# A cached-attention and MLP decode kernel: a folded weight's two halves loaded at the very first on two queues, and one scalar put behind the last gelu

## The chip, the cores and the metric

The kernel runs on one core of a Trainium2 chip. Its engines are TensorE (PE, with its weight loads listed apart as PEld), VectorE (DVE), ScalarE (ACT), GpSimd (POOL) and SyncE (SP), and 16 DMA engines carry what the queues of SP and ACT issue. The metric is the device time of one execution in microseconds; lower is better. Before the change three runs took 1078.3, 1078.7 and 1079.33 us, median 1078.7 us.

## The reference, cut to what matters

Two layers are run, each an attention block A followed by an MLP block B, with the same weights in both layers. There are 8 rows (batch), one token each, width D = 448, 16 query heads over 8 key/value heads, 4096 cached positions of 256 elements, all bf16:

```python
x = A_x
x = x + _A_ref(_layernorm(x), A_k_cache, A_v_cache, A_wq, A_wo)
x = x + _B_ref(_layernorm(x), B_w1, B_w2, B_w3, B_w4)
x = x + _A_ref(_layernorm(x), A_k_cache, A_v_cache, A_wq, A_wo)
x = x + _B_ref(_layernorm(x), B_w1, B_w2, B_w3, B_w4)
```

`_A_ref` forms q = x @ wq, scores against the K cache, softmax over 4096 positions, the sum over the V cache, and `@ wo`. In `_B_ref` the token is one position long, so every shifted part of the first mixer is zero and `x1 = x`; what is left is `x + gelu(layernorm(x) @ w3) @ w4` with w3 of 448 x 1792 and w4 of 1792 x 448. The K and V caches together are 268 MB; each row's 33.5 MB are needed by both layers.

## The kernel before, in words

Each of the 64 (row, head) pairs has a K tile and a V tile of 2 MB, cut in four units of 512 KB ("u" 0 to 3, one SBUF slot each, 30 slots in all). A front (`front`) loads a K tile, transposes it on TensorE (L1509), copies it back (DVE L1440 or ACT L1441), takes the scores (L1148, L1405) and does the softmax; a back (`back`) loads the V tile, multiplies (L1275), sums the partial rows (L1311) and applies wo (L1339, L1086). Some units of heads 3 to 7 are kept in SBUF from layer 0 to layer 1; all others are read a second time. Row b+1's layer 0 is interleaved with row b's layer 1, and `mid` runs row b's layer-0 MLP in between. The first six rows share one MLP of the second layer; the last two rows have a last one at the very end (`mlp` with `dst is None`), whose output `last_rows` forms and stores.

The order of everything is worked out on the host by a planner, `Plan.schedule`. It is a list scheduler with a modelled duration for every operation: at each step the engine that can begin first takes its ready operation of the lowest `prio`. It gives slots to the K and V units and joins neighbouring units into one transfer of up to 2 MB; a transfer waits on its queue until the last reader of every slot that it overwrites is done. In gaps of TensorE's plan it puts filler matmuls (listed at L1716), so many that a modelled count of recent columns stays under a target. After it `synchronise` derives the semaphore waits. So a changed duration or dependency moves later decisions of the plan too.

Transfers on the SP queue go in order of `prio`. K and V units count 0, 1, 2, ... as they are called for; the constant weights stand between them by `at`:

```python
def dma_once(name, parts, keys, at, also=()):
    for i, (dst, src, nbytes, *row) in enumerate(parts):
        dma(name, dst, src, nbytes, nc.alloc_semaphore(f"s_{name}{i}"), 16,
            [keys[i], *(also if i == 0 else ())], 4 * at - 0.5, *row)
```

448 rows of a weight are three blocks of 128 and one of 64. The fourth block of wq and of w3 is folded: its left half of columns stands in partitions 0 to 63 of one tile and its right half in partitions 64 to 127 (`wqx_sb`, `w3x_sb`). Before the change the order on SP is: x, the left half of wqx, two K tiles, wq, more K and V, wo, K and V, and at `at` = 18 w3's three blocks and both halves of w3x (two transfers of 112 KB, L628), then V units and w4. The right half of wqx is the only load issued by ACT's queue, at the start (L1575). Who reads w3x: `column_sums_h` (L917, once, with the mask as the other operand) and the first product of every MLP (L917).

At the end of the last MLP (DVE): L1031 and L1033 form the argument of tanh, ACT does tanh (L1037), L1046 forms gelu times two (`hT`), which TensorE multiplies with w4 (L973). Beside it `last_scale(1)` works out two scalars of the last row's residual (L828; L830 and L836), with which L965 scales the residual `xs`; L979 adds the product and `xs`, and two transfers store the rows (L982).

Of the kernel before, what the change touches and what calls it, by code (L numbers as in the profile page):

```python
# [6 lines left out]
P = 128  # L7
B = 8
D = 448
# [466 lines left out]
def bass_interleave_layers__gqa_block_cached__mixer_s_mlp__decode_kernel(  # L476
# [20 lines left out]
    plan = Plan()  # L497
# [6 lines left out]
    def sb(name, shape, dt):  # L504
        n = 4 if dt in (f32, i32) else 2
        for s in shape[1:]:
            n *= s
        al = 32 if n >= 128 else 8
        cursor[0] = (cursor[0] + al - 1) // al * al
        t = nc.alloc_sbuf_tensor_at(name, shape, dt, offset=cursor[0], align_bytes=al)  # L510
        cursor[0] += (n + al - 1) // al * al
        assert cursor[0] <= high0, (name, cursor[0], high0)
        return t
# [5 lines left out]
    w3x_sb = sb("w3x_sb", [P, F // 2], bf)  # L519
# [31 lines left out]
    lin = sb("lin", [P, 2, 2], f32)  # L551
# [5 lines left out]
    hT = sb("hT", [P, NB], bf)  # L557
# [67 lines left out]
    def dma(name, dst, src, nbytes, sem, val, wr, at, row=8192):  # L625

        us = nbytes / 16 / 26.88e3 + nbytes / row / 16 * 0.008
        plan.op("sp", lambda eng: eng.dma_start(dst, src), us / FASTER, name, wr=wr, prio=at,  # L628
                dma=(sem, val))
# [6 lines that stand above are left out]
# [49 lines left out]
    def const_c(v):  # L685
# [7 lines left out]
            wr=["sel"])  # L693
# [7 lines left out]
    for bank, key in [(psR, "R"), (psM, M)]:  # L701
        plan.op("dve", lambda v, bank=bank: v.memset(bank[:, :], 0.0), 0.5, "const",
                wr=["psM", ("row", 0), ("row", 1)], banks=[key])
# [7 lines left out]
    def dv(fn, dur=0.13, rd=(), wr=(), banks=(), name="chain", prio=None):  # L711
        if prio is None:
            prio = urge[0] + len(plan.ops)
        return plan.op("dve", fn, dur, name, rd=rd, wr=wr, banks=banks, prio=prio)
# [71 lines left out]
    def factor(k, c, v, rd, dv=dv):  # L786


        x, t, y = (z[:, k, c:c + 1] for z in (var, rst, rsy))
        a, b = (KK * (1.0 + LN_EPS) / D, KK * LN_EPS * LN_EPS) if k else (KK / D, KK * LN_EPS)  # L790
        dv(lambda e: e.tensor_scalar(x, v, a, b, ALU.mult, ALU.add), rd=rd, wr=[("x", k, c)])
        newton(x, t, y, ("t", k, c), [("x", k, c)], ("y", k, c), dv)
# [26 lines left out]
    def last_scale(r):  # L819


        c = B - 2 + r
        y, sf = rsy[:, 0, c:c + 1], self_f[:, r:r + 1]
        mm = mom[:, 2, 4 * r + 1:4 * r + 2]
        if r == 0:
            factor(0, c, mom[:, 2, 4 * r:4 * r + 1], [("v", r)])
        add = self_f[:, 0:1] if r == 0 else lin[:, 0, 0:1]
        dv(lambda v: v.tensor_scalar(lin[:, r, 0:1], y, sf, add, ALU.mult, ALU.add),  # L828
           rd=[("y", 0, c), "sel_f"] + [("lin", 0, 0), "hT"] * r, wr=[("lin", r, 0)])
        dv(lambda v: v.tensor_scalar(lin[:, r, 1:2], y, sf, mm, ALU.mult, ALU.mult),  # L830
           rd=[("y", 0, c), ("mm", r), "sel_f"], wr=[("lin", r, 1)])
        if r == 0:
            dv(lambda v: v.tensor_tensor(lin[:, 0, 0:1], lin[:, 0, 0:1], self_f[:, 1:2], ALU.add),
               rd=[("lin", 0, 0), "sel_f"], wr=[("lin", 0, 0)])
        else:
            dv(lambda v: v.tensor_tensor(lin[:, 1, 1:2], lin[:, 1, 1:2], lin[:, 0, 1:2], ALU.add),  # L836
               rd=[("lin", 0, 1), ("lin", 1, 1)], wr=[("lin", 1, 1)])
# [148 lines left out]
    def mlp(src, skey, n, dst, dkeys, rows_open=False):  # L986
# [62 lines left out]
        if dst is None:  # L1049
            last_scale(1)  # L1050
            return last_rows(src, skey, n)
# [518 lines left out]
    def load_wq():  # L1570
        dma_once("wq", [(wq_sb[:, kc, :], A_wq[kc * P:(kc + 1) * P, :], 1 << 20)
                        for kc in range(3)], ["wq0", "wq1", "wq2"], 2)
        dma_once("wqx", [(wqx_sb[0:64, :], A_wq[384:D, 0:2048], 1 << 19)], ["wqx0"], 0.05)
        s_wqx = nc.alloc_semaphore("s_wqx1")
        plan.op("act", lambda a: a.dma_start(wqx_sb[64:P, :], A_wq[384:D, 2048:4096]), 0.1, "wqx1",  # L1575
                wr=["wqx1"], prio=0, dma=(s_wqx, 16))

    def load_rest():
        dma_once("wo", [(wo_sb[:, :].rearrange("p (t n) -> p t n", n=2 * D),
                         A_wo.rearrange("(t m c) n -> m t (c n)", m=P, c=2), 3670016, 1792)], ["wo0"], 6)  # L1580
        dma_once("w3", [(w3_sb[:, kc, :], B_w3[kc * P:(kc + 1) * P, :], 458752)
                        for kc in range(3)], ["w30", "w31", "w32"], 18)
        dma_once("w3x", [(w3x_sb[0:64, :], B_w3[384:D, 0:896], 114688 * 2),
                         (w3x_sb[64:P, :], B_w3[384:D, 896:1792], 114688 * 2)], ["w3x0", "w3x1"], 18)
    def load_w4():
        w4s = B_w4.rearrange("(s f) n -> s f n", s=2)
        dma_once("w4", [(w4_sb[:, 7 * i * D:(7 * i + 6) * D].rearrange("p (t n) -> p t n", n=2 * D),
                         w4s[i, 0:768].rearrange("(t m c) n -> m t (c n)", m=P, c=2), 688128, 1792)
                        for i in range(2)] +
                 [(w4_sb[:, (7 * i + 6) * D:(7 * i + 7) * D], w4s[i, 768:896], 114688, 896)  # L1590
                  for i in range(2)], ["w40", "w41", "w42", "w43"], 20, ["xr0", "xr1", "xr2"])
# [58 lines left out]
    def with_first_results(k, b):  # L1650
# [15 lines left out]
        run(k[MLP_TO:])  # L1666

    load_wq()
    load_rest()
    first_queries()  # L1670
    load_w4()
# [6 lines left out]
    for b in range(B):  # L1678
        kf = {"K": l2_heads[:], "F": free_heads[:]}
        order2 = [kf[c].pop(0) for c in MIX] if b < B - 2 else l2_heads + free_heads  # L1680
        first = QFIRST if b < B - 1 else QLAST
        mid(b, order2[:first])
        q_todo[b] = order2[first:]
        first2[b] = order2[0]
        if b < B - 1:
            run([("b", 0, b + 1, h) for h in free_heads])
        if b < B - 2:
            run(both(1, b, order2))
            with_first_results(both(0, b + 1, kept_heads, [(0, b + 2, h) for h in free_heads]), b)
        elif b == B - 2:  # L1690
            k = both(1, b, l2_heads)
            k.remove(("b", 1, b, l2_heads[-1]))
            run(k)
            with_first_results(both(0, b + 1, kept_heads, [(1, b, h) for h in free_heads]), b)
        else:
            k = both(1, b, l2_heads, [(1, b, h) for h in free_heads], AT=LAST_AT)
            for h, at in zip(l2_heads[-1:] + free_heads, BACKS):
                k.insert(at, ("b", 1, b - 1, h))
            run(k[:STAT_AT])
            urge[0] = 0  # L1700
            last_stats(0)
            last_scale(0)
            urge[0] = CH
            run(k[STAT_AT:] + [("b", 1, b, h) for h in free_heads])
# [71 lines left out]
```

## Time and profile before

| What | Value |
|---|---|
| Three runs | 1078.3, 1078.7, 1079.33 us |
| The profiled execution: its time, its span | 1076.9 us, 1075.1 us |
| Busy: PE, PEld, DVE, ACT, POOL | 88%, 60%, 55%, 32%, 9% |
| DMA traffic | 436.39 MB, mean 406 GB/s |
| Mean granted TensorE clock | 0.935 |
| Filler matmuls L1716 into psP (x359) | 57.8 us busy, 288 ns each |

The page of the profile cuts the span in 40 slices; "DMA" in tenths is the mean busy share of the 16 DMA engines, "GB/s" what they moved. A query by windows gives one row a stretch: its start and end, its length, busy us and count of PE, PEld, DVE, ACT and POOL, the granted TensorE clock, the DMA share and GB/s. The timeline gives an instruction's start, its duration, engine, line and operands. A busy share of 1.0 says that the DMA engines always had a packet in hand, not that the packets went at their best rate. The profiled execution was 1.8 us faster than the median of the three.

### The profile page before, as it was taken

What the parts mean: (1) busy time and instruction counts of PE and PEld (TensorE: products, weight loads), DVE (VectorE), ACT (ScalarE), POOL (GpSimd) and SP (SyncE); (2) the same over time, 40 slices, a digit from 0 to 9 for tenths busy, and PEclk for the clock granted to TensorE, in tenths of its full rate; (3) what the DMA queues carried; (4) which work ended last, traced back from release to release, by engine and by line L of the source; (5) the groups of instructions that cost most, each with busy time, mean ns of one, the idle gap of its engine ahead of it and who ended that gap; (6) DMA issues with size and microseconds to landing.
All of it is one profiled execution on the core that took longest, in us unless ns stands there. A gap on an engine that the chain in (4) does not pass through costs nothing.

```text
span 1075.1 us, 34110 instructions
## 1 busy us (share of the span) xinstructions
PE 943.7 (88%) x15206; PEld 649.6 (60%) x15206; DVE 588.3 (55%) x1879; ACT 343.7 (32%) x946; POOL 99.6 (9%) x284
## 2 busy tenths in 40 slices
PE   4989798898989989898989889998898899998996
PEld 4556555565656656566566655666555676666574
DVE  4345455555555556555565555555555656566474
ACT  1235113341234403254133431334223441343140
POOL 0000010010100101011010100100011000111011
PEclk9799899998999989999899998999999988999696
DMA  9999999999999999999999999999999999999995
GB/s 353 408 425 424 390 407 424 424 422 402 406 424 426 417 400 420 425 426 403 387 424 426 424 413 399 425 425 424 396 408 424 426 393 394 397 423 416 329 426 232
DMA packets 56526, 436.39 MB, mean 406 GB/s; under 512 B 6062, under 2 KB 9276, under 8 KB 34236
## 3 DMA queue, kind: packets, MB, share of 16 engines
q1 hardware_dynamic: 56292, 433.95, 98.4%
q8 instruction: 119, 1.95, 0.7%
q10 hardware_dynamic: 88, 0.26, 0.1%
q14 instruction: 27, 0.22, 0.1%
HBM read 434.18 MB, written 0.01 MB: 404 GB/s over the span
## 4 chain that ended last, share of the span: by engine, by line
DMA 56%; PE 36%; DVE 3%; SPq 2%; issue 1%; ACT 1%; POOL 0%; DVEq 0%
DMA kv<-in_A_k_cache_dram 32%; DMA kv<-in_A_v_cache_dram 23%; PE psT L1509 12%; PE psP L1275 7%; PE psT L1405 5%; PE psM L1148 3%; PE psR L1339 2%; SPq L628 2%; PE psM L1065 1%; PE psM L901 1%; DVE kv L1440 1%; DMA w_sb<-in_B_w_dram 1%; PE psP L1716 1%; PE psM L917 1%; SPq L645 1%
## 5 line engine op out<-in xcount | busy, mean ns | idle before, releaser
L1509 PE MATMUL psT<-ident_f,kv 128*128 128x128 f32 x2752 | 373.8, 283 | 37.1 <-DMA kv<-in_A_k_cache_dram 35.6
L1509 PEld LDWEIGHTS psT<-ident_f,kv 128*128 128x128 f32 x2752 | 301.6, 143 | 117.6 <-issue 54.9
L1440 DVE COPY kv<-psT 128x512 f32<-128x512 f32 x368 | 253.1, 691 | 196.8 <-PE psT L1509 189.2
L1441 ACT COPY kv<-psT 128x512 f32<-128x512 f32 x352 | 205.0, 586 | 386.9 <-PE psT L1509 301.9
L1275 PE MATMUL psP<-kv,pT 128*2 128x256 bf16 x4032 | 175.6, 290 | 18.8 <-DMA kv<-in_A_v_cache_dram 16.3
L1405 PE MATMUL psT<-kv,qz 128*32 128x512 bf16 x1664 | 133.7, 396 | 3.0 <-ACT kv L1441 1.9
L1275 PEld LDWEIGHTS psP<-kv,pT 128*2 128x2 bf16 x4032 | 81.7, 83 | 63.4 <-DMA kv<-in_A_v_cache_dram 25.6
L1228 POOL PARTITION_ALL_REDUCE gm<-pm x128 | 45.5, 355 | 772.7 <-DVE pm L1226 762.9
L1238 ACT ACTIVATE pT<-sS,nb,fac 128x32 bf16<-128x32 bf16 x128 | 52.6, 417 | 116.7 <-DVE nb L1232 116.7
L1301 DVE CAST oS<-psP 128x256 bf16<-128x256 f32 x126 | 53.3, 423 | 52.6 <-PE psP L1275 51.1
L1339 PE MATMUL psR<-wo_sb,oT 128*1 128x448 bf16 x444 | 62.6, 366 | 7.7 <-DVE oT L1318 4.0
L1242 POOL PARTITION_ALL_REDUCE Db<-rs x128 | 51.0, 398 | 182.9 <-ACT pT L1238 182.9
L1311 PEld LDWEIGHTS psP<-sel,oS 128*128 128x128 bf16 x504 | 23.0, 98 | 60.5 <-DVE oS L1303 54.4
L1311 PE MATMUL psP<-sel,oS 128*128 128x2 bf16 x504 | 31.8, 166 | 31.4 <-DVE oS L1303 29.4
L1238 ACT ACTIVATE pT<-sS,nb 128x32 bf16<-128x32 bf16 x128 | 40.8, 326 | 54.9 <-DVE nb L1232 54.9
L1716 PE MATMUL psP<-ident_f 128*128 128x256 bf16 x359 | 57.8, 288 | 0.0
L1405 PEld LDWEIGHTS psT<-kv,qz 128*32 128x32 bf16 x1664 | 34.5, 95 | 36.6 <-issue 13.3
L1420 DVE CAST sr<-psT 128x512 bf16<-128x512 f32 x55 | 38.0, 692 | 31.7 <-PE psT L1405 31.5
L1303 DVE TENSOR_TENSOR oS<-psP,oS 128x256 bf16<-128x256 f32 x126 | 53.3, 423 | 2.9
L1148 PEld LDWEIGHTS psM<-qz,kv 128*128 128x128 bf16 x1344 | 42.5, 100 | 17.2 <-issue 7.5
L1148 PE MATMUL psM<-qz,kv 128*128 128x48 bf16 x1344 | 49.5, 189 | 3.2 <-issue 1.3
L1421 ACT CAST sr<-psT 128x512 bf16<-128x512 f32 x49 | 28.7, 585 | 54.0 <-PE psT L1405 51.0
(197 smaller groups left out, 786.8 us busy)
## 6 DMA issues: line engine op xcount, KB each, us to landing
kv<-in_A_k_cache_dram SPq DMA_DIRECT2D x68, 2048.0 KB, 23.3
kv<-in_A_v_cache_dram SPq DMA_DIRECT2D x61, 2048.0 KB, 17.4
kv<-in_A_v_cache_dram SPq DMA_DIRECT2D x163, 512.0 KB, 8.3
kv<-in_A_k_cache_dram SPq DMA_DIRECT2D x12, 1536.0 KB, 17.7
kv<-in_A_k_cache_dram SPq DMA_DIRECT2D x28, 512.0 KB, 9.1
kv<-in_A_v_cache_dram SPq DMA_DIRECT2D x14, 1024.0 KB, 8.8
kv<-in_A_v_cache_dram SPq DMA_DIRECT2D x7, 1536.0 KB, 11.1
kv<-in_A_k_cache_dram SPq DMA_DIRECT2D x8, 1024.0 KB, 9.5
```

The costliest lines, as they stand in the source:

```text
L1148: last = t.matmul(ps[:, SB + 2 * i:SB + 2 * i + 2 * REP], a()[:, c:256:2], bcast(rhs(c), REP, 1), start=(c == 0), stop=(c == 1))
L1238: return a.activation(pT[nr][:, :, :].rearrange("p i j -> p j i")[:, jj, :], sview[:, jj, :], ACT.Exp, bias=nb[nm][:, jj:jj + 1], scale=sc ...
L1275: last = t.matmul(ps[g4:g4 + 2, PV0:PV0 + DH], pT[nr][:, k, :], slot_ap(q, s * 256, 256), start=(i < 4), stop=(i >= 28), skip_group_check= ...
L1301: plan.op("dve", lambda v: v.tensor_copy(oS[:, 0, :], po), 0.36, "o", rd=[("pv", par, x) for x in range(4)], wr=["oS0"], banks=[bk], prio=hi)
L1303: plan.op("dve", lambda v: v.tensor_tensor(oS[:, 1, :], po, oS[:, 0, :], ALU.subtract), 0.36, "o", rd=["oS0"] + [("pv", par, x) for x in r ...
L1311: last = t.matmul(ps[:, PV1 + 2 * c:PV1 + 2 * c + 2], oS[:, w, c:DH:2], sel[:, :], start=(w == 0), stop=(w == 1))
L1339: last = t.matmul(psR[r:r + 1, 0:D], oT[no][:, i % 2, i // 2:i // 2 + 1], wo_sb[:, a:a + D], start=(k == 1 and i < 2), stop=(k == turn_at ...
L1405: last = t.matmul(psT[bank][32 * g:32 * g + 32, :], qz[:, a:a + 32], slot_ap(qs[g // 2], g % 2 * 1024, 1024)[:, c:1024:2], start=(half == ...
L1440: return e.tensor_copy(dst, psT[bank][:, :])
L1441: return e.copy(dst, psT[bank][:, :])
L1509: last = t.transpose(psT[bank][:, s * P:(s + 1) * P], src, ident_f[:, :])
L1716: return t.matmul(dst, ident_b, bcast(ident_b[:, 0:n // 4], 4, 1), start=True, stop=True)
```

## The change

In its first part w3x's left half moves on the SP queue from behind w3 to right behind the left half of wqx, ahead of the first K tile, and its right half moves to ACT's queue, behind the right half of wqx. The bytes that the planner counts for the halves (they set its modelled duration) fall from 229,376 each to 114,688 for the left; the right half is modelled as 0.1 us of ACT. In its second part L830 of the last row (r = 1) may no longer be placed before `hT`; L828 of that row already had this dependency. Nothing else in the source changes, but the planner's order does: in the listing of the changed kernel's instructions the SP queue has other piece sizes at many places, 41 fewer filler matmuls stand on TensorE (391 for 432), and some 25 copies have changed sides between DVE and ACT.

```diff
@@ last_scale
         dv(lambda v: v.tensor_scalar(lin[:, r, 1:2], y, sf, mm, ALU.mult, ALU.mult),
-           rd=[("y", 0, c), ("mm", r), "sel_f"], wr=[("lin", r, 1)])
+           rd=[("y", 0, c), ("mm", r), "sel_f"] + ["hT"] * r, wr=[("lin", r, 1)])
@@ load_wq
         plan.op("act", lambda a: a.dma_start(wqx_sb[64:P, :], A_wq[384:D, 2048:4096]), 0.1, "wqx1",
                 wr=["wqx1"], prio=0, dma=(s_wqx, 16))
+        dma_once("w3x", [(w3x_sb[0:64, :], B_w3[384:D, 0:896], 114688)], ["w3x0"], 0.06)
+        s_w3x = nc.alloc_semaphore("s_w3x1")
+        plan.op("act", lambda a: a.dma_start(w3x_sb[64:P, :], B_w3[384:D, 896:1792]), 0.1, "w3x1",
+                wr=["w3x1"], prio=1, dma=(s_w3x, 16))
@@ load_rest
-        dma_once("w3x", [(w3x_sb[0:64, :], B_w3[384:D, 0:896], 114688 * 2),
-                         (w3x_sb[64:P, :], B_w3[384:D, 896:1792], 114688 * 2)], ["w3x0", "w3x1"], 18)
```

## The prediction

> **What bounds the kernel now.** I read the page first: its chain of waits and its DMA queues.
>
> ```profile
> DMA packets 56526, 436.39 MB, mean 406 GB/s; under 512 B 6062, under 2 KB 9276, under 8 KB 34236
> q1 hardware_dynamic: 56292, 433.95, 98.4%
> q10 hardware_dynamic: 88, 0.26, 0.1%
> DMA 56%; PE 36%; DVE 3%; SPq 2%; issue 1%; ACT 1%; POOL 0%; DVEq 0%
> ```
>
> SP's queue (q1) holds the 16 DMA engines 98.4% of the span; q10 (ACT's) carries almost nothing. So the time is the stream of 434 MB, plus a head before it and a tail of about 11 us behind its last bytes (4 to 8 GB/s after 1064 us). Whatever lets the stream run below its good rate costs time one for one; other work is paid only in the tail. Next the windows, for the stretches where w3x lands and where the new loads will go (last column GB/s, before it the DMA share).
>
> ```profile
> 2.00:4.00 2.00, 0.00 (x0) 0.00 (x0) 1.18 (x10) 0.62 (x1) 0.29 (x1) 1.00 0.84 222
> 4.00:6.00 2.00, 0.99 (x32) 0.93 (x33) 0.18 (x1) 0.00 (x0) 0.00 (x0) 1.00 1.12 254
> 6.00:8.00 2.00, 0.40 (x15) 0.31 (x12) 1.39 (x10) 0.00 (x0) 0.00 (x0) 1.00 0.70 246
> ...
> 110.00:112.00 2.00, 2.00 (x34) 1.89 (x33) 1.34 (x3) 1.23 (x3) 0.00 (x0) 1.00 1.00 416
> 112.00:114.00 2.00, 1.53 (x39) 1.08 (x38) 1.38 (x2) 0.00 (x0) 0.00 (x0) 1.00 0.95 379
> 114.00:116.00 2.00, 1.54 (x40) 0.90 (x36) 1.30 (x5) 0.33 (x3) 0.35 (x1) 1.00 1.08 370
> 116.00:118.00 2.00, 1.72 (x15) 0.71 (x15) 1.14 (x5) 0.39 (x4) 0.40 (x1) 1.00 1.09 296
> 118.00:120.00 2.00, 0.31 (x12) 0.34 (x13) 0.06 (x1) 0.00 (x0) 0.00 (x0) 0.77 1.03 376
> ```
>
> w3x is issued at 107.0 and 107.5 us and lands 12.1 us later, so its packets fly in the last of these rows. The engines are busy (share 1.03 to 1.09), yet move 296 and 376 GB/s: packets are slow, not missing. At the start, where the halves of wqx are in flight, the rate is 222 to 254. Third, the stretches between one row's tanh (L1037) and the next: the same work under five different pieces of the plan.
>
> ```profile
> 132.28:263.09 130.81, 114.86 (x1822) 77.88 (x1821) 71.24 (x223) 43.09 (x119) 12.05 (x32) 0.97 1.01 417
> 263.09:391.01 127.92, 113.97 (x1812) 77.22 (x1810) 71.10 (x223) 42.95 (x120) 12.04 (x32) 0.95 1.01 415
> 391.01:521.19 130.18, 115.33 (x1831) 78.06 (x1834) 72.16 (x226) 42.48 (x117) 12.04 (x32) 0.95 1.01 415
> 521.19:649.00 127.81, 113.55 (x1818) 78.79 (x1810) 72.34 (x224) 42.72 (x119) 12.05 (x32) 0.97 1.01 415
> 649.00:777.00 128.00, 114.03 (x1813) 78.64 (x1813) 73.05 (x225) 42.26 (x117) 12.04 (x32) 0.95 1.01 416
> ```
>
> They last 127.8 to 130.8 us, but each at 415 to 417 GB/s: the long ones only moved more bytes ahead. A new order of the same work in the middle is thus worth little: 1 GB/s in 415 of 128 us is 0.3 us. Last, the tail, in order of time:
>
> ```profile
> 1070.26 0.16 DVE L800 TENSOR_SCALAR mom<-psR 128x1 f32<-128x1 f32 x1
> 1070.52 0.27 DVE L830 TENSOR_SCALAR lin<-rsy,self_f,mom 128x1 f32<-128x1 f32 x1
> 1070.71 0.18 DVE L1046 SCALAR_TENSOR_TENSOR hT<-g,hb 128x28 bf16<-128x28 f32 x1
> 1072.47 0.27 DVE L979 SCALAR_TENSOR_TENSOR o_last<-psM,xs 128x112 bf16<-128x112 f32 x1 [0.77 <-PE psM L973]
> ```
>
> **The change part by part.**
>
> *w3x leaves 105 to 120 us.* Its 229,376 bytes at 420 GB/s (about what the neighbouring rows reach) are 0.55 us. If the slowness of the stretch goes with it, the rows 116 to 120 give back ((420-296)+(420-376)) x 2/420 = 0.80 us; with 112 to 116 too, where w3's 448 KB blocks fly, another (41+50) x 2/420 = 0.43 us. Ends: 0.55 and 1.78 us saved. I take 1.57, between 1.35 and 1.78, since the dip is sharp and stands where w3x is.
>
> *The column sums* (L917, 119.7 us) waited 1.9 us for w3x; they will wait for w3's third block, issued just before it. TensorE was not the bound there: no price, covered by the stream.
>
> *w3x arrives at 2 to 8 us.* It costs its bytes at the rate that rules there. Lowest: 0.27 us (the left half alone at 420, the right hidden beside it). Highest: all 229,376 bytes at 240 GB/s, 0.96 us. I take 0.60: the left half, in line ahead of the K tiles, at 246 GB/s is 0.47, and half of the right one's 0.27. K's first tile lands that much later and TensorE's first transposes (12.67 us) begin later; the queue is filled many tiles ahead then (one SP issue lasts 33.9 us from 12.77 us), so only the bytes count. One more issue on SP (w3x's took 0.54 us each) stands ahead of K's issue at 2.13 us, while the queue still has wqx in flight. On ACT one issue stands ahead of the table load at 1.34 us; ACT's first copy is at 16.39 us. The sum of this move is -1.57 + 0.60 = -0.97 us.
>
> The Trainium skill speaks against the two halves helping each other: "SBUF — State Buffer", Can I just issue two DMAs to hit both halves?, says that two transfers to opposite partition halves gained only 6% over one, and Door 1 gives 64 partitions about 218 GB/s. By it the start would cost an estimated 229,376/218,000 = 1.05 us and the move would bring 0.52 us instead of 0.97. The trace agrees on the rate (222 to 254 GB/s); it shows no two halves side by side for long.
>
> *L830 behind hT.* Tanh starts at 1070.26. In the row MLPs hT starts 0.24 to 0.25 us after tanh starts (132.28 to 132.52, 263.09 to 263.34); here 0.45, with L830 ahead of it. So hT starts 0.19 us sooner, less 0.02 for a tanh of 0.23 for 0.21 us. The scalars (0.27, 0.27, 0.16 us) and xs (0.39) then lie beside TensorE's 1.48 us of L973; L979 had waited 0.77 us for it, so the cover holds. In the new order of DVE one t_h (L796) also comes ahead of an hb (L996): up to 0.06 us lost. I take -0.15; ends -0.19 and 0.
>
> *The order anew.* 364 K and V transfers for 361: smaller pieces at 134 to 140 us ran at 408 to 419 GB/s against 420 to 430, some 0.06 us a 512 KB unit; I take +0.1. Middle stretches: 0, ends -1 and +1 (five times 0.3, partly cancelling). The last rows' stage is priced in the rivals.
>
> Sum: -0.97 - 0.15 + 0.1 = -1.0. The profiled execution (1076.9, span 1075.1, 1.8 around it) would become 1075.9; it lies 1.8 below the median, and from the median 1078.7 - 1.0 = 1077.7 us.
>
> **Rivals.**
>
> *The new order starves the last stage less (faster).* Around the seventh row MLP and the last one's the stream starves:
>
> ```profile
> 996.00:1000.00 4.00, 3.48 (x91) 2.48 (x92) 2.82 (x22) 0.00 (x0) 0.00 (x0) 0.54 0.87 325
> 1000.00:1004.00 4.00, 4.00 (x99) 2.65 (x89) 1.12 (x5) 0.22 (x1) 0.00 (x0) 0.50 0.95 260
> ...
> 1008.00:1012.00 4.00, 3.13 (x54) 1.90 (x54) 1.01 (x3) 0.00 (x0) 0.00 (x0) 0.50 0.85 289
> ```
>
> Six rows from 996 to 1020 (325, 260, 360, 289, 332, 349) lose 605 x 4/420 = 5.8 us. Nowhere does the plan matter more, and the V pieces ahead of it change (2 MB, 1 MB, 1 MB for twice 1.5 MB). A third less loss is -1.9: 1075.8 us. For: the pieces do differ. Against: TensorE runs at half clock there, whatever the order.
>
> *Fewer fillers, longer half clock (slower).* 391 fillers for 432, mostly 6 to 13 fewer a row. Around each row's MLP the clock column falls to 0.50 for some 12 us (260 to 272: 389, 388, 381 GB/s). One 4 us row more of it in eight stages, at (415-389)/415 x 4 = 0.25 us, is 2.0, and two rows more in the last stage, at 4 x (420-308)/420 = 1.07 each (308 is the mean of its four half-clock rows), 2.1: 1077.7 + 4.1 = 1081.8 us. It decides once the added dips pass 3.2 us. Against: fillers are placed in planned gaps, so fewer may mean fewer gaps, and with them the five stretches kept 415 to 417.
>
> *The move is neutral*: the slowness belongs to wherever 64-partition loads fly and is paid again at the start. Saved 1.35, paid 0.96 and the dip's 0.80 again: +0.4, with the tail and pieces 1079.1 us.
>
> **Chances.** 0.2% is 2.2 us, about what a measurement of this kernel can tell from no change: below 1076.5 is faster, above 1080.9 slower. The forecast (0.46) has 0.14 of it below 1076.5, from the full 1.78, the cheap start and a good middle. Better last stage 0.24, all faster. Neutral 0.11, all within. Fillers 0.19, of which 0.18 beyond 1080.9 and 0.01 within. So faster 0.38, same 0.44, slower 0.18. Range: the better last stage by half (5.8/2 on -1.0, and -0.5 of middle) gives 1074.3, the fillers' case 1081.8; I set 1074.0 to 1082.0. The forecast's own range is 1075.7 to 1079.0.
>
> **What would show it.** Rates of 400 or more at 112 to 120 us and the column sums waiting for w3 alone: first step right; a dip of that depth elsewhere: wrong. A start at or below 250 GB/s for about 0.6 us longer, transposes from about 13.2 us. hT 0.25 us after tanh. Stretches between tanhs at 415 to 417 GB/s. The forecast is wrong if 996 to 1020 loses much other than 5.8 us, or if half-clock stretches grow.

## The result, and the profile after

The changed kernel took 1075.18 us (median of 6 runs, 1073.41 to 1076.73) against 1078.5 us before (6 runs, 1077.42 to 1079.33): ratio 0.9974, 95% interval 0.9963 to 0.9984, or 2.8 us (1.7 to 4.0). Beside the first set of experiments, against 35 runs of before, it was 0.9985 (0.9969 to 1.0001). Single executions of one and the same kernel spread by 4 to 10 us there (the 35 of before lay between 1073.7 and 1081.5), so a term of a microsecond is read from the traces below, stretch by stretch, and not from one time.

The profiled execution of the changed kernel happened to be the slowest of its six (1076.73 us, span 1074.9), and the one of before (1076.9, span 1075.1) was faster than all three of its unprofiled runs. Their spans show no gain (0.2 us); single stretches differ. The page, queues and chain:

```profile
DMA packets 56958, 436.39 MB, mean 406 GB/s; under 512 B 6110, under 2 KB 9324, under 8 KB 34284
q1 hardware_dynamic: 56644, 433.84, 98.3%
q10 hardware_dynamic: 168, 0.38, 0.2%
DMA 54%; PE 37%; DVE 5%; SPq 2%; issue 1%; ACT 1%; POOL 0%
```

ACT's queue (q10) now carries 0.38 MB for 0.26: the right half of w3x. The bound is what it was, the stream. The windows of the changed kernel (last column GB/s, before it the DMA share, before that the granted clock):

```profile
2.00:4.00 2.00, 0.00 (x0) 0.00 (x0) 1.18 (x10) 1.26 (x1) 0.29 (x1) 1.00 0.92 205
4.00:6.00 2.00, 0.59 (x17) 0.54 (x18) 0.18 (x1) 0.00 (x0) 0.00 (x0) 1.00 1.25 295
6.00:8.00 2.00, 0.80 (x30) 0.71 (x27) 1.06 (x8) 0.00 (x0) 0.00 (x0) 1.00 0.90 377
...
112.00:114.00 2.00, 1.81 (x52) 1.40 (x50) 0.90 (x3) 0.56 (x1) 0.00 (x0) 1.00 1.00 393
114.00:116.00 2.00, 0.61 (x16) 0.29 (x16) 0.74 (x4) 0.00 (x0) 0.35 (x1) 1.00 1.06 430
116.00:118.00 2.00, 1.42 (x13) 0.52 (x13) 1.14 (x5) 0.72 (x4) 0.40 (x1) 1.00 1.08 455
118.00:120.00 2.00, 1.61 (x58) 1.60 (x58) 0.47 (x2) 0.00 (x0) 0.00 (x0) 1.00 1.00 408
```

The dip of 296 and 376 GB/s at 116 to 120 us is gone (455 and 408), and the column sums no longer stop TensorE for it. The same stretches between one row's tanh and the next now read:

```profile
263.92:393.75 129.83, 114.61 (x1808) 76.91 (x1808) 71.86 (x224) 41.92 (x117) 12.05 (x32) 0.93 1.00 411
393.75:520.61 126.86, 114.22 (x1805) 81.14 (x1805) 75.49 (x229) 39.70 (x114) 12.04 (x32) 0.93 1.01 417
647.94:779.17 131.23, 116.27 (x1825) 79.70 (x1826) 74.75 (x230) 40.02 (x113) 12.05 (x32) 0.92 1.00 412
```

The five are at 411 to 417 GB/s (414 and 415 in the two not shown). They show no effect of the new order: in another execution under the order of before (the run with the tail alone, below) they read 414, 411, 416, 414 and 416. The last stage of the row MLPs is the one around the eighth row's tanh (at 1001 us before, 1003 us here; the prediction calls it the seventh). Here the kernel before fell to 260 to 360 GB/s with the clock at 0.50 to 0.54. The changed kernel:

```profile
996.00:1000.00 4.00, 3.36 (x81) 2.63 (x82) 1.95 (x14) 0.00 (x0) 0.00 (x0) 0.80 0.97 383
1000.00:1004.00 4.00, 3.28 (x80) 1.98 (x77) 2.57 (x17) 0.21 (x1) 0.00 (x0) 0.77 0.95 337
1004.00:1008.00 4.00, 4.00 (x96) 3.07 (x93) 1.31 (x6) 0.00 (x0) 0.00 (x0) 0.66 1.00 377
1008.00:1012.00 4.00, 4.00 (x87) 2.63 (x85) 1.66 (x12) 0.00 (x0) 0.00 (x0) 0.50 0.99 365
```

It starves less in this profile: from 996 to 1020 us it loses 3.1 us against 420 GB/s, by the prediction's count, for 5.8. In a second profile of the changed kernel the dip is as deep but shorter, and the same count gives 4.2 us:

```profile
996.00:1000.00 4.00, 4.00 (x97) 3.04 (x94) 3.10 (x23) 0.00 (x0) 0.00 (x0) 0.50 0.88 333
1000.00:1004.00 4.00, 3.60 (x98) 2.61 (x94) 0.99 (x7) 0.21 (x1) 0.00 (x0) 0.93 0.83 248
1004.00:1008.00 4.00, 4.00 (x82) 2.41 (x75) 2.69 (x16) 0.00 (x0) 0.00 (x0) 0.63 0.94 285
1008.00:1012.00 4.00, 2.67 (x96) 2.30 (x93) 0.85 (x3) 0.59 (x1) 0.00 (x0) 1.00 1.01 398
```

Since the stage comes a little earlier or later in each execution, it is better compared over 41 us placed by its tanh: before, the changed kernel, and the changed kernel's second profile.

```profile
985.00:1026.00 41.00, 35.19 (x742) 22.55 (x744) 21.35 (x89) 5.20 (x18) 2.26 (x6) 0.79 0.96 359
987.00:1028.00 41.00, 34.41 (x749) 23.23 (x748) 20.25 (x88) 5.76 (x19) 2.26 (x6) 0.88 0.99 386
984.00:1025.00 41.00, 33.70 (x730) 22.79 (x729) 19.58 (x87) 5.22 (x18) 2.26 (x6) 0.88 0.98 376
```

And the tail, from the timeline of DVE; tanh starts at 1070.29 us here:

```profile
1070.29 0.16 DVE L800 TENSOR_SCALAR mom<-psR 128x1 f32<-128x1 f32 x1
1070.55 0.19 DVE L1046 SCALAR_TENSOR_TENSOR hT<-g,hb 128x28 bf16<-128x28 f32 x1
1071.04 0.27 DVE L830 TENSOR_SCALAR lin<-rsy,self_f,mom 128x1 f32<-128x1 f32 x1
1072.32 0.27 DVE L979 SCALAR_TENSOR_TENSOR o_last<-psM,xs 128x112 bf16<-128x112 f32 x1 [0.33 <-PE psM L973]
```

hT begins 0.26 us behind tanh (0.45 before), and L979 2.03 us behind it (2.21 before): 0.18 us.

### The profile page after: what moved, and what is told of

Its sections match the earlier page's. It is cut to its first block, busy times and chain, and to the rows that moved or that the text cites. A ratio compares the mean times of both kernels' runs of the same rounds, so it can differ in the third digit from the quotient of the medians.

```text
span 1074.9 us, 34022 instructions
## 1 busy us (share of the span) xinstructions
PE 943.2 (88%) x15165; PEld 653.4 (61%) x15165; DVE 602.5 (56%) x1904; ACT 329.3 (31%) x921; POOL 99.6 (9%) x284
## 4 chain that ended last, share of the span: by engine, by line
DMA 54%; PE 37%; DVE 5%; SPq 2%; issue 1%; ACT 1%; POOL 0%
DMA kv<-in_A_k_cache_dram 29%; DMA kv<-in_A_v_cache_dram 23%; PE psT L1509 12%; PE psP L1275 8%; PE psT L1405 4%; PE psM L1148 3%; PE psR L1339 2%; PE psM L1065 2%; SPq L628 1%; PE psM L901 1%; DVE oS L1303 1%; DVE oS L1301 1%; PE psP L1718 1%; DVE kv L1440 1%; DMA w_sb<-in_B_w_dram 1%
## 5 line engine op out<-in xcount | busy, mean ns | idle before, releaser
L1509 PE MATMUL psT<-ident_f,kv 128*128 128x128 f32 x2752 | 380.0, 286 | 29.0 <-DMA kv<-in_A_k_cache_dram 27.1
L1509 PEld LDWEIGHTS psT<-ident_f,kv 128*128 128x128 f32 x2752 | 307.6, 145 | 111.9 <-issue 57.4
L1440 DVE COPY kv<-psT 128x512 f32<-128x512 f32 x388 | 264.9, 690 | 180.1 <-PE psT L1509 172.0
L1441 ACT COPY kv<-psT 128x512 f32<-128x512 f32 x332 | 193.4, 586 | 395.7 <-PE psT L1509 314.7
L1420 DVE CAST sr<-psT 128x512 bf16<-128x512 f32 x61 | 42.2, 692 | 32.4 <-PE psT L1405 32.2
L1718 PE MATMUL psP<-ident_f 128*128 128x256 bf16 x319 | 52.4, 288 | 0.0
L1221 DVE CAST sS<-psM 128x64 bf16<-128x64 f32 x128 | 28.0, 219 | 34.9 <-PE psM L1148 24.1
```

What stands on the lines that cost most here:

```text
L1440: return e.tensor_copy(dst, psT[bank][:, :])
L1441: return e.copy(dst, psT[bank][:, :])
L1509: last = t.transpose(psT[bank][:, s * P:(s + 1) * P], src, ident_f[:, :])
L1718: return t.matmul(dst, ident_b, bcast(ident_b[:, 0:n // 4], 4, 1), start=True, stop=True)
```

## The experiments

All keep the computation whole. Most hold the planner's order fixed: a few lines put in after `plan.schedule()` take the two w3x transfers out of their queues and put them elsewhere, and the waits are derived afresh. So the move and the new order can be tried apart. Ratios are times over those of the kernel before, run beside it; 0.001 is 1.1 us. The diffs are cut to the lines that matter: `sp` and `act` are the planner's lists of SP and ACT, and `left` and `right` the two transfers of w3x.

**The move alone, under the order of before** (run twice).

```diff
     plan.schedule()
+    left, right = [o for o in sp if o.name == "w3x"]
+    sp.remove(left); sp.remove(right)
+    sp.insert([o.name for o in sp].index("wqx") + 1, left)
+    act.insert([o.name for o in act].index("wqx1") + 1, right); right.eng = "act"
```

> The order of the kernel before is kept instruction for instruction; only the two loads of w3x are taken from behind w3 and put where the change puts them (left half behind the left half of wqx on SP, right half on ACT's queue). Theory M (the move itself brings the time): at 120 us the stream is 1 to 1.6 us of bytes ahead, and the time is 1.5 to 2.5 us below the kernel before, ratio 0.9977 to 0.9986. Theory N (the new order of the plan brings it, most of it around the last row MLPs): the early lead is given back in the first MLP stage and the time is within 0.7 us of before, ratio 0.9994 to 1.0003.

> The old order with w3x early on both queues, once more. Twice (two queues, one queue) the old order with an early w3x gained 1.1 us at 100 to 122 us and then lost 4.9 and 5.0 us around the second row MLP (247 to 288 us), against 2.5 to 3.5 in the eight others. If the old order gives the gain back there for a reason, this profile loses 4.5 or more there and the ratio is 0.9995 to 1.0015. If that was chance, it loses about 3 and the ratio is 0.9985 to 0.9995.

Measured: ratio 1.0000 (0.9984 to 1.0016), and 0.9991 (0.9973 to 1.0008) the second time. The dip went both times: 100 to 122 us ran at 414 and 412 GB/s, where the orders with a late w3x ran at 386 to 392. The windows of the first of the two:

```profile
0.00:20.00 20.00, 9.22 (x85) 8.70 (x85) 8.76 (x34) 3.56 (x5) 1.58 (x22) 1.00 0.90 339
100.00:122.00 22.00, 19.67 (x326) 14.21 (x323) 11.79 (x33) 7.38 (x22) 2.27 (x6) 1.00 1.01 414
122.00:160.00 38.00, 32.07 (x715) 21.20 (x716) 18.52 (x83) 4.99 (x17) 2.62 (x7) 0.91 1.02 387
988.00:1029.00 41.00, 33.81 (x709) 21.20 (x709) 20.59 (x87) 4.93 (x17) 2.26 (x6) 0.83 0.93 354
```

Theory M's time did not come: its move brings the early gain, but no time clear of the interval. The first ratio is theory N's, the second lies between the two. The last stage is as bad as with the late w3x. Around the second row MLP (247 to 288 us) this one and the one-queue kernel below ran at 378 and 377 GB/s, against 392 to 400 in four other kernels of the old order; but the repeat ran at 393, so giving the gain back there is no fixed property of the order.

**The new order alone, with w3x back behind w3** (run twice).

```diff
     plan.schedule()
+    sp.remove(left); act.remove(right); right.eng = "sp"
+    at = max(i for i, o in enumerate(sp) if o.name == "w3") + 1
+    sp[at:at] = [left, right]
```

> The order of the changed kernel is kept; only the two loads of w3x go back behind w3 on SP. Theory M: the dip of 116 to 120 us returns (300 to 380 GB/s) and with it the time, to within 1 us of the kernel before, ratio 0.999 to 1.000. Theory N: the dip returns but the time keeps most of the gain, 2 to 3 us below before, ratio 0.9972 to 0.9982.

> The new order with both loads of w3x behind w3, once more. If the gain of the changed kernel is the sum of two parts, the dip at 100 to 122 us (1.1 us) and the new order's shorter loss in the last stage (about 1.5 us), this kernel keeps the second: ratio 0.9982 to 0.9992, the last stage loses 4 to 5.5 us and 100 to 122 us loses 1.8. If the new order only pays with w3x early, the ratio is 0.9995 to 1.0010 as in the first time (1.0001).

Measured: 1.0001 (0.9982 to 1.0020) and 0.9988 (0.9972 to 1.0004). The dip is back (389 and 390 GB/s at 100 to 122 us) while the last stage keeps the new order's rate (373 and 384). Theory N's 2 to 3 us did not come; the first ratio is theory M's, the second fits a sum of two parts. The second of them:

```profile
100.00:122.00 22.00, 16.81 (x293) 12.41 (x294) 11.43 (x32) 5.88 (x20) 2.26 (x6) 0.97 1.01 390
987.00:1028.00 41.00, 33.09 (x726) 22.47 (x726) 18.95 (x86) 5.38 (x18) 2.26 (x6) 0.88 0.99 384
```

**The parts of the source, and the changed kernel again.** One kernel has the added `["hT"] * r` alone, one has all but it:

> The kernel before with the second part of the change alone: the last row's second residual scalar stands behind hT; all other engines and queues keep their order. hT starts 0.26 us behind the tanh of 1070 us instead of 0.45, and the time is 0.15 us below before (0.1 to 0.2), which a ratio of 0.9998 plus or minus its interval can't tell from 1. A theory in which the tail matters for the measured gain wants 1 us or more, ratio 0.999.

> The changed source without its second part: w3x at the start and the new order that follows from it, the last row's scalar left where it was. So far three profiles of the new order lost 4.0, 5.1 and 5.3 us in the last stage (about 985 to 1026 us) and three of the old order 6.7, 5.5 and 7.2. If the new order is what helps there, this profile loses 4 to 5.5 us; if those differences are chance, anything from 4 to 7. Time as the changed kernel's plus 0.15 us: ratio 0.997 to 0.9995.

> The changed kernel itself beside the others on one chip: ratio 0.9963 to 0.9984 as measured. Its one profiled execution so far was the slowest of six (1076.7 us), so another is wanted for the stretches: all theories expect the early lead of 0.7 us at 10 us and 1.6 us at 120 us again; theory N expects 996 to 1020 us to lose some 3 to 4 us rather than 5.8; a theory of luck expects stretches that differ from profile to profile without order.

Measured: the tail alone 1.0002 (0.9989 to 1.0015), with every other engine's order unchanged; hT stood 0.26 us behind tanh (1069.31 for 1069.05) and L979 2.03 us, as in the changed kernel. All but the tail: 0.9983 (0.9968 to 0.9999), the last stage at 381 GB/s, 4.3 us lost, as expected of the new order. The changed kernel: 0.9985 (0.9969 to 1.0001), the last stage at 376. The early lead of 0.7 us at 10 us, which all theories expected, was no property of the change: the first 20 us ran at 330 GB/s in this execution, 340 in the first, and 324 to 347 with the loads of before.

**Where the price lies: w3x in the middle of the stream.** Under the order of before, both halves on SP ahead of wo:

```diff
+    at = [o.name for o in sp].index("wo")
+    sp.insert(at, left); sp.insert(at + 1, right)
```

> The order of the kernel before; both halves of w3x on SP, one behind the other, ahead of wo, in the middle of the stream of 2 MB tiles (some 35 us after the start). Theory P (a dip of 1.1 us belongs to the 64-partition loads wherever they fly between other loads): the stretch from 20 to 100 us, which lost 1.2 to 1.3 us against 426 GB/s in all six profiles so far, loses 2.2 to 2.5, and 100 to 122 us falls from 1.85 to about 0.7, so nothing is gained. Theory Q (the dip belongs to the place, with w3's 3.5 KB rows and the start of the MLP stage): 20 to 100 us keeps its 1.2 to 1.3 and the 1.1 us are gained. In the time 1 us is 0.001 of the ratio.

Measured: ratio 0.9998 (0.9984 to 1.0012). Its windows:

```profile
40.00:42.00 2.00, 2.00 (x27) 1.21 (x29) 1.36 (x5) 1.18 (x6) 0.40 (x1) 1.00 1.00 395
42.00:44.00 2.00, 1.46 (x44) 0.81 (x36) 1.10 (x4) 1.10 (x2) 0.00 (x0) 1.00 0.97 208
44.00:46.00 2.00, 1.68 (x48) 1.36 (x46) 0.94 (x5) 0.53 (x3) 0.35 (x1) 1.00 1.05 286
...
20.00:100.00 80.00, 68.91 (x902) 45.06 (x900) 33.02 (x89) 25.76 (x68) 6.04 (x16) 0.89 1.02 413
100.00:122.00 22.00, 19.33 (x319) 14.02 (x319) 11.37 (x33) 7.76 (x23) 2.26 (x6) 1.00 1.01 416
```

And the same stretches of the kernel before:

```profile
42.00:44.00 2.00, 2.00 (x48) 1.51 (x47) 0.88 (x4) 0.71 (x3) 0.40 (x1) 1.00 0.87 345
44.00:46.00 2.00, 1.14 (x30) 0.70 (x23) 1.40 (x5) 0.58 (x1) 0.10 (x1) 1.00 1.04 384
46.00:48.00 2.00, 2.00 (x63) 1.70 (x63) 0.38 (x3) 0.72 (x4) 0.66 (x2) 0.85 1.06 381
...
0.00:20.00 20.00, 8.49 (x86) 7.92 (x86) 8.88 (x34) 3.63 (x5) 1.58 (x22) 1.00 0.86 324
20.00:100.00 80.00, 69.85 (x916) 47.82 (x920) 33.97 (x91) 26.14 (x68) 6.05 (x16) 0.89 1.01 421
100.00:122.00 22.00, 18.30 (x311) 13.24 (x305) 10.98 (x31) 7.38 (x22) 2.26 (x6) 0.93 1.01 392
```

The dip moved with the loads: theory P. 20 to 100 us, at 421 GB/s in all thirteen other profiles, fell to 413, which is 80 x 8/426 = 1.5 us, for the 1.2 us or so that 100 to 122 us got back. So these two loads cost the stream more than their bytes at both places in it where they were tried.

Two other readings lie near. One is the length of their rows, 1,792 bytes. But wo, the transfer right behind them here, has rows of that length too (in the source, pieces of 896 bf16 elements) and fills all 128 partitions, and while it flew (about 46.6 to 55.9 us by the landings) the windows of 2 us ran at 372 to 432 GB/s, not at 208 or 286. So row length alone doesn't make the dip. The other is their small size of 112 KB each; no run parts it from the 64 partitions.

The lowest row, 208 GB/s with the engines busy (0.97), lies near the 218 GB/s that the Trainium skill, "SBUF — State Buffer", Door 1, gives for 64 partitions, which reach half the ports. That rate covers only part of the price: by it the 229,376 bytes would take an estimated 1.05 us, 0.5 us more than at 420 GB/s, and the stretches lost 1.2 and 1.5 us more. Where the rest comes from no run here shows.

**Two queues or one, at the start.** Under the order of before and under the new one, both halves on SP one behind the other:

```diff
+    sp.insert(at, left); sp.insert(at + 1, right)   # at: behind "wqx"
```

> The order of the kernel before; both halves of w3x at the very first, but one behind the other on SP's queue, ahead of the first K tile. If the two queues matter, the first 20 us lose more than with a half on each (4.4 to 5.4 us against 426 GB/s in six profiles, mean 4.8): the halves alone at about 240 GB/s would add 0.4 to 0.5 us. If only the place matters, 0 to 20 us stays at 4.4 to 5.4 and 100 to 122 us falls to about 0.75.

> The changed kernel with both halves of w3x at the start on SP's queue, one behind the other; all else in the changed kernel's order. If the second queue is worth nothing, the time is the changed kernel's: ratio 0.9974 to 0.9985. If the second queue matters, 0.4 to 0.5 us more than that, ratio 0.9980 to 0.9990, and 0 to 20 us loses more than the 4.3 to 5.4 us of all profiles so far.

Measured: 1.0013 (0.9998 to 1.0029) under the old order, 0.9984 (0.9967 to 1.0001) under the new. The first 20 us ran at 339 and 330 GB/s; with a half on each queue at 339, 334, 340, 330 and 340, and at 335 under the third order below. The old order's row beside the one of two queues above:

```profile
0.00:20.00 20.00, 8.94 (x85) 8.51 (x85) 8.68 (x33) 3.33 (x5) 1.58 (x22) 1.00 0.89 339
100.00:122.00 22.00, 19.80 (x328) 14.20 (x326) 11.77 (x33) 7.38 (x22) 2.26 (x6) 1.00 1.01 414
```

The second queue is worth nothing that shows, in the start's rate or in the time; the ratios alone, with intervals of some 0.0016 either way, could not tell the 0.4 to 0.5 us in question. That agrees with the Trainium skill, "SBUF — State Buffer", Can I just issue two DMAs to hit both halves?, which gives a gain of only 6% for two transfers to opposite halves.

**The fillers.** The order of before without its 432 filler matmuls:

```diff
+    plan.order["pe"] = [o for o in plan.order["pe"] if o.name != "warm"]
```

> The order of the kernel before without its 432 filler matmuls, all else in its order. The rival of fewer fillers says that the half-clock stretches around each row's MLP grow and the stream starves longer: 391 fillers for 432 is a tenth of that step, so if that rival bites, none of them costs several us, 3 to 10, ratio 1.003 to 1.009. If fillers hardly matter here, the ratio is 0.998 to 1.002, and 41 fewer are nothing.

Measured: 1.0013 (1.0000 to 1.0025), 1.4 us (0 to 2.7) for all 432. The mean granted clock fell with them:

```profile
core 0: 1077.9 us, clock 0.881
```

against 0.935 before. If each filler were worth the same, a tenth of them would be some 0.14 us. The rival's mechanism doesn't show either: around the first row MLP, without fillers (first row) and before (second row), the clock is lower by 0.20 and the stream is no slower.

```profile
122.00:160.00 38.00, 31.33 (x692) 20.60 (x694) 18.80 (x84) 5.11 (x19) 2.61 (x7) 0.70 1.03 407
122.00:160.00 38.00, 34.05 (x727) 22.24 (x728) 19.38 (x86) 4.91 (x17) 2.62 (x7) 0.90 1.02 402
```

**A third order.** The changed source, with 229,376 bytes counted for the left half as before the change: other decisions throughout, the same early loads.

> The changed source, but the planner counts 229,376 bytes for the left half of w3x, as it did before the change; the same work and the same early loads under a third order. If the gain is that of an early w3x under an order planned for it, the ratio is that of the changed kernel, 0.9970 to 0.9987. If a large part of the gain is the luck of one order (most of all in the last stage), the ratio lies anywhere from 0.997 to 1.001 and the last stage's loss between 4 and 8 us goes with it.

Measured: 0.9988 (0.9969 to 1.0007), between the two theories and wide enough for both. 100 to 122 us ran at 409 GB/s and the last stage at 378, as in the changed kernel (386 and 376); the stretch in between, 122 to 160 us, at 379, lower than any other.

**The stretches of all fourteen profiles.** From windows as above, loss counted against 426 GB/s (the good rate of the 2 MB stretches), as length x (difference of mean rates)/426:

| Stretch | Mean GB/s | Mean GB/s | Difference |
|---|---|---|---|
| 0 to 20 us | w3x late 342 (six: 324 to 347) | w3x early 336 (eight: 330 to 340) | 0.3 us lost, not clear |
| 100 to 122 us | late 389 (five: 386 to 392) | early, without the third order, 413 (seven: 411 to 414) | 1.2 us gained |
| 122 to 160 us | late 396 (five: 387 to 407) | early 390 (eight: 379 to 400) | 0.6 us lost, not clear |
| 16 us before to 25 us after the eighth row's tanh | old order 361 (seven: 345 to 372) | new order 379 (six: 373 to 386) | 1.7 us gained |
| from there to 7 us before the last tanh | old order 0.55 to 1.65 us lost, mean 1.1 | new order 1.2 to 2.0, mean 1.7 | 0.6 us lost, ranges overlap |

In the fourth row no profile of the old order reaches the lowest of the new one, though the gap is narrow (372 and 373). What in the new order helps there is not shown: the clock of that stretch is 0.88 in all six of the new order, but under the old one 372 GB/s came with 0.88 and 371 with 0.79. In the third row the old order against the new gives the same 396 and 390, so that loss can belong to the order as well as to the early w3x. w3x's bytes (0.55 us) are paid in one place for the other. The tail gives 0.18 us. The sum, -1.2 + 0.3 + 0.6 - 1.7 + 0.6 - 0.2, is -1.6 us; the kernels with the new order and an early w3x measured 0.9974, 0.9985, 0.9983 and 0.9984, -1.6 to -2.8 us. That the two meet may be chance. The table leaves out most of the span: from 160 us to 16 us before the eighth row's tanh, by windows of 4 us, the profiles lost 21 to 27 us, a spread several times any term of the sum (before 22.6, the changed kernel 24.6 and 21.1). The move under the old order (1.0000, 0.9991, 1.0013) and the new order with a late w3x (1.0001, 0.9988) show no gain clear of their intervals; whether the two need each other beyond their sum stays open, as the intervals of plus or minus 1.7 us hold the sum of parts as well.

## Why the prediction was right or wrong

The forecast was 1077.7 us, a gain of 1.0 us; it measured 2.8 (1.7 to 4.0), at 1075.2 us, just below the forecast's own range of 1075.7 to 1079.0 and inside the full range of 1074.0 to 1082.0. The direction was right, the size came out short. Measured again the gain was 1.6 us (0.9985), so part of the 2.8 may be chance. The term that made up nearly all of the forecast, the move of w3x, is seen in its stretches but not in the time: alone under the order of before it measured 1.0000, 0.9991 and, on one queue, 1.0013. How near the forecast came is therefore in part luck.

- *w3x leaves 105 to 120 us*: right by the stretch. 1.57 us was taken; the dip's 1.2 and the bytes' 0.55 are 1.77, at the upper end of the 0.55 to 1.78.
- *w3x arrives at 2 to 8 us*: 0.60 was taken; 0.55 for the bytes and 0.3 of slower start, which is not clear of the spread, are 0.85, inside 0.27 to 0.96. The net, -0.97 as forecast, is -0.9 by the stretches.
- *The Trainium skill's rule on two halves* ("SBUF — State Buffer", Can I just issue two DMAs to hit both halves?): it held on its own ground, since one queue served as well as two. The estimate of 1.05 us for the start, worked out from the 218 GB/s of Door 1, is a little above the 0.85, and the spread of the start does not tell the two apart.
- *The tail*: 0.15 taken, 0.18 measured in the trace; the cover held, L979 still waited 0.33 us for L973.
- *The order anew, and the last stage left to a rival*: this is the step that fell short. The sum put the last stage at 0 and left a third of its loss, 1.9 us, to the rival of the better last stage (0.24). That rival came in: 1.7 us there, of which 0.6 is lost again right behind it. The working had the place and the size; the weight was too small. Its reason against, half clock there whatever the order, did not hold: the mean clock of the stage was 0.79 to 0.88 with the old order and 0.88 with the new, and rows of the changed kernel had 0.80, 0.77 and 0.66. Its reason for, the other pieces of V, was not tried alone. The forecast's own sign of being wrong, a loss from 996 to 1020 us much other than 5.8, came in: 3.1 and 4.2 us. The +0.1 for smaller pieces rests on a range of 408 to 419 GB/s at 134 to 140 us; windows of 2 us there read 414, 408 and 385, and no run shows the term alone.
- *Fewer fillers*: wrong at its root. All 432 fillers together are worth 1.4 us (0 to 2.7), while the rival put 4.1 us on 41 of them.
- *The neutral rival* was half right: the dip does follow the load (208 GB/s in the stream), but at the start the stretches show 0.3 us instead of the 0.80 it expected there. In the time its result, no gain, is what the move alone gave under the order of before.
- *The middle stretches* at 415 to 417 GB/s were read as proof that order is worth under 1 us. Over all fourteen profiles they read 407 to 417, 411 to 416 in another execution of the old order, and a stretch of 41 us ran at 377 to 400 under that order; five stretches of one execution had shown too narrow a spread.

Against the listing of what would show it: 112 to 120 us at 393, 430, 455 and 408 (forecast 400 or more; right but for the first), hT 0.26 us behind tanh (forecast 0.25), and the transposes began at 11.7 us in the changed kernel's first profile and at 12.9 in its second (12.7 before), not at 13.2: the start varies from one execution to the next by more than the 0.6 us.

## What to carry to other kernels

In this kernel two small loads of 64 partitions slowed a saturated stream by more than their bytes, at both places tried. Look for a place where the stream is not yet at its rate, measure whether the time follows, and don't count on a second queue for the other half. Where a planner rewrites the whole order after a small edit, price the places where the stream already starves, not the mean, and hold the order fixed to tell the edit from its echo. When single executions spread by more than the term sought, compare the same stretch over many profiles.

## What the runs showed that was not expected

The same kernel's executions spread over 0.7% (1073.7 to 1081.5 us for before). In the last stage the granted clock of the old order was 0.54, 0.50, 0.50 and 0.50 from 996 to 1012 us in one execution; the mean over the stretch was 0.79 to 0.88 with the old order, and 0.88 with the new one each time. And 229 KB of 64-partition loads cost the stream 1.2 to 1.5 us beyond their 0.55 us when they flew amid other loads, and some 0.3 us, not clear of the spread, in the first 20 us.
